# Linear attention beside a mixture of experts: numerators copied by ScalarE and multiplied by GpSimd, key-sum tails behind the queries' projection, eight steps a pair

## The chip, the cores and the metric

The kernel runs on one core of a Trainium2 chip. The metric is the time of one execution on the device in microseconds (us), as the median of several runs. One execution was also profiled; durations below come from that one.

## What is computed

```python
def _attn_ref(q, k, v, omega):                 # q, k, v: 4 x 8 heads x 576 x 64; omega: 128 x 64
    scale = 1.0 / np.sqrt(np.sqrt(D))
    def phi(x):
        h = np.einsum('bhsd,md->bhsm', x, omega) - np.sum(x * x, axis=-1, keepdims=True) / 2.0
        h = h - np.max(h, axis=-1, keepdims=True)
        return np.exp(h) / np.sqrt(m)
    q_p, k_p = phi(q * scale), phi(k * scale)
    kv = np.einsum('bhsm,bhsd->bhmd', k_p, v)  # key sums, and z: the same with ones for v
    num = np.einsum('bhsm,bhmd->bhsd', q_p, kv)
    den = np.einsum('bhsm,bhm->bhs', q_p, z)[..., None] + 1e-06
    return num / den

def _moe_ref(x, domain_probs, w1, w2):         # x: 2304 tokens x 512; 4 experts, 1024 hidden
    p = domain_probs / (domain_probs.sum(-1, keepdims=True) + 1e-09)
    for e in range(E):
        out += p[:, e:e + 1] * (np.maximum(x @ w1[e], 0.0) @ w2[e])
```

The 8 heads go in pairs, so there are 4 pairs a batch and 16 in all. A sequence of 576 is four tiles of 128 and a tail of 64.

## The kernel before

Attention and expert work are interleaved by hand: the order in the code is the order on every engine's queue. `emit` goes through the experts' visits (`plain`, later `fast`), and after each half tile of expert work it takes as many steps of an attention generator as a rate in `windows` says. The first batch is done by `Pair`; the twelve pairs of batches 1 to 3 by `Halves`. `later_ticks(pairs, over)` yields the steps of these: with `over` true for the eight pairs of batches 1 and 2, which run beside visit 3 up to N0 (76 steps for 45.4 shares of expert work), with `over` false for the four pairs of batch 3, beside the `fast` visits.

One pair of `Halves`, in before, takes nine steps. `project("k")` and `project_tails` (64-row matmuls, two heads in the two halves of the array, tiles k_ps and t_ps) come with `maxima`; then maxima of the tails, `bias` (nbk, from the squared lengths of `lengths` and the maxima) and `exp("k", 0)`; then `exp("k", 1)` and `exp_tails("k")`; then `project("q")` (q_ps); then the exponentials of the queries; then `sum_keys` (kv: one matmul for both heads' tails, 128 rows by 256 columns, and eight of 128 columns on the full tiles, then the parts kvh and kvl); then two steps of `turn` (transposes, qt_ps, into qth and qtl). With `over`, the `numerators` and `divide` of a pair are called in the first steps of the next pair (`before`): part 0 has 256 tokens a head, part 1 has 320. `numerators` makes numerator and denominator of a head in one PSUM tile nd, 64 partitions each, and ScalarE copies the denominators to dn; `divide` takes the reciprocal on VectorE and multiplies there, straight from nd, into raw_x, the experts' input.

All PSUM tiles come from one pool of eight banks (`bank`); a new tile waits until the bank that it gets has been read for the last time. nd needs one bank for part 0, two for part 1; k_ps, t_ps and q_ps two each; kv one; g of the experts one each.

ScalarE also makes the high parts of the split weights (w1sh, w1ah, w2h, sum), the relu hh and some of the accumulations; VectorE makes hl, the low part of the hidden values, and the accumulation acc; GpSimd makes the low parts of the weights and the squares of k and q. In the text, the pairs of the window with `over` count from the first to the eighth.

## Time and profile before

| | |
|---|---|
| median of 3 runs | 915.62 us (915.03 to 915.73) |
| the profiled execution | 915.08 us, span of its instructions 913.3 us |
| TensorE (PE) busy | 900.7 us, 99% |
| VectorE (DVE) busy | 556.7 us, 61% |
| ScalarE (ACT) busy | 433.3 us, 47% |
| GpSimd (POOL) busy | 378.6 us, 41% |
| PE waits, 58 to 276 us | 3.7 us in 6 waits |

A matmul's record ends later than the next begins, since they are pipelined; so how long PE spends on a kind of matmul is read from start to start. The idle time that the profile shows in brackets or in the list of waits begins at the modelled end of the matmul before. What releases a waiting instruction is named with its engine and line.

### The profile page before, as it was taken

To read this page: it belongs to the slowest core of one execution; us is meant where nothing else is said; L and a number is where in the kernel's file an instruction comes from. 1 tells how busy PE (TensorE), PEld (TensorE's weight loads), DVE (VectorE), ACT (ScalarE), POOL (GpSimd) and SP (SyncE) were. 2 spreads that over 40 slices of the span, in tenths; PEclk is the share of its full clock that TensorE was granted. 3 is DMA by queue.
4 is the path that set the end of the run, shared out by engine and by line. 5 is a ranking of instruction groups with operands and counts; after the bars stand their busy time and mean duration, and the time that the engine had idled before them with its cause. 6 is when DMAs were issued, how large, how long until landed. Compare 5 with 4: busy or idle time off the path is not lost.

```text
span 913.3 us, 13234 instructions
## 1 busy us (share of the span) xinstructions
PE 900.7 (99%) x4908; PEld 781.1 (86%) x4908; DVE 556.7 (61%) x946; ACT 433.3 (47%) x964; POOL 378.6 (41%) x296
## 2 busy tenths in 40 slices
PE   9999999999999999999999999999999999999998
PEld 9888888888777888888888889888888888898886
DVE  5755676777779655575757574886344545534543
ACT  6454665565664555445254445254544243342340
POOL 5756453444533453324344333344334343434330
PEclk9999999999999999999999999999999999999999
DMA  7663454444511612204122111214112112122102
GB/s 180 179 204 120 133 156 144 151 133 139 171 56 37 189 60 86 81 24 138 42 78 93 55 47 47 70 47 150 51 42 81 50 55 70 47 69 59 34 12 81
DMA packets 47360, 83.56 MB, mean 91 GB/s; under 512 B 8704, under 2 KB 17088, under 8 KB 47296
## 3 DMA queue, kind: packets, MB, share of 16 engines
q1 hardware_dynamic: 47056, 82.43, 29.9%
q8 instruction: 38, 0.62, 0.3%
q10 hardware_dynamic: 240, 0.30, 0.1%
q14 instruction: 26, 0.21, 0.1%
HBM read 77.99 MB, written 4.72 MB: 91 GB/s over the span
## 4 chain that ended last, share of the span: by engine, by line
PE 88%; DVE 7%; ACT 3%; issue 1%; DVEq 0%; ACTq 0%
PE g L713 28%; PE g L597 13%; PE g L599 13%; PE g L598 13%; PE g L582 3%; PE g L584 3%; PE g L583 3%; PE kv L316 2%; PE k_ps L265 1%; PE qt_ps L327 1%; PE k_ps L147 1%; ACT kp L298 1%; DVE dn L365 1%; PE kv L177 1%; PE q_ps L147 1%
## 5 line engine op out<-in xcount | busy, mean ns | idle before, releaser
L597 PE MATMUL g<-w2h,hh 128*128 128x512 f32 x536 | 212.4, 396 | 1.0 <-DVE raw_x L369 1.0
L599 PE MATMUL g<-w2h,hl 128*128 128x512 f32 x536 | 209.8, 391 | 1.2 <-DVE hl L589 1.2
L598 PE MATMUL g<-w2l,hh 128*128 128x512 f32 x536 | 209.0, 390 | 0.0
L494 POOL TENSOR_TENSOR w2l<-w2r,w2h 128x512 fp32r<-128x512 f32 x93 | 122.4, 1320 | 206.9 <-ACT w2h L491 145.9
L494 POOL TENSOR_TENSOR w1sl<-w1r,w1sh 128x1024 fp32r<-128x1024 f32 (+1 forms) x59 | 113.4, 1922 | 153.5 <-ACT w1sh L491 141.9
L610 DVE SCALAR_TENSOR_TENSOR acc<-g,pr,acc 128x512 f32<-128x512 f32 x126 | 93.7, 748 | 74.6 <-PE g L599 73.9
L724 DVE TENSOR_TENSOR sum<-g,sum 128x448 f32<-128x448 f32 x96 | 59.7, 622 | 117.7 <-PE g L713 110.1
L494 POOL TENSOR_TENSOR w1al<-w1r,w1ah 128x256 fp32r<-128x256 f32 (+1 forms) x77 | 82.5, 1090 | 110.3 <-ACT w1ah L491 110.3
L599 PEld LDWEIGHTS g<-w2h,hl 128*128 128x128 f32 x536 | 100.6, 188 | 24.5 <-DVE hl L589 2.4
L597 PEld LDWEIGHTS g<-w2h,hh 128*128 128x128 f32 x536 | 100.7, 188 | 21.1 <-PE nd L357 1.2
L598 PEld LDWEIGHTS g<-w2l,hh 128*128 128x128 f32 x536 | 100.8, 188 | 18.4
L725 ACT ACTIVATE hh<-sum 128x448 fp32r<-128x448 f32 x96 | 55.5, 578 | 121.9 <-DVE sum L724 121.9
L726 DVE SCALAR_TENSOR_TENSOR hl<-sum,hh 128x448 fp32r<-128x448 f32 x96 | 61.9, 644 | 61.9 <-ACT hh L725 61.9
L491 ACT ACTIVATE w1sh<-w1r 128x1024 fp32r<-128x1024 f32 (+1 forms) x59 | 51.0, 864 | 98.6 <-DVE w1r L548 98.4
L713 PE MATMUL g<-xbh,w1sh 128*128 128x448 f32 x256 | 93.6, 366 | 0.7 <-ACT sum L719 0.5
L713 PE MATMUL g<-xbl,w1sh 128*128 128x448 f32 x256 | 93.7, 366 | 0.0
L713 PE MATMUL g<-xbh,w1sl 128*128 128x448 f32 x256 | 93.4, 365 | 0.0
L719 ACT ACTIVATE sum<-g 128x448 f32<-128x448 f32 x96 | 51.7, 541 | 56.5 <-PE g L713 56.4
L713 PE MATMUL g<-xbh,w1ah 128*128 128x448 f32 x192 | 70.6, 367 | 0.9 <-ACT kp L298 0.9
L713 PE MATMUL g<-xbh,w1al 128*128 128x448 f32 x192 | 70.2, 366 | 0.0
L713 PE MATMUL g<-xbl,w1ah 128*128 128x448 f32 x192 | 70.1, 365 | 0.0
L491 ACT ACTIVATE w2h<-w2r 128x512 fp32r<-128x512 f32 x90 | 55.5, 624 | 8.8 <-issue 4.8
(161 smaller groups left out, 1603.8 us busy)
## 6 DMA issues: line engine op xcount, KB each, us to landing
w1r<-in_w SPq DMA_DIRECT2D x54, 512.0 KB, 3.7
w2r<-in_w SPq DMA_DIRECT2D x108, 256.0 KB, 2.6
out<-acc SPq DMA_DIRECT2D x18, 256.0 KB, 2.6
va<-in_vn SPq DMA_DIRECT2D x14, 256.0 KB, 4.1
k<-in_kd SPq DMA_DIRECT2D x12, 288.0 KB, 3.7
k<-in_kn SPq DMA_DIRECT2D x12, 288.0 KB, 4.3
q<-in_qd SPq DMA_DIRECT2D x12, 288.0 KB, 4.5
q<-in_qn SPq DMA_DIRECT2D x12, 288.0 KB, 4.8
```

The lines of the kernel that those rows point to most:

```text
L491: hi.activation(a, t, AF.Copy)
L494: lo.tensor_tensor(c, t, f32(a), ALU.subtract)
L582: nc.tensor.matmul(ps[:, :n], a[:, w], hi, start=(hp == 0), stop=False)
L597: nc.tensor.matmul(ps, ha[:, ts_], wa, start=(c == 0), stop=False)
L598: nc.tensor.matmul(ps, ha[:, ts_], wc, start=False, stop=False)
L599: nc.tensor.matmul(ps, hc[:, ts_], wa, start=False, stop=(c == FH - 1))
L610: nc.vector.scalar_tensor_tensor(acc[i], ps, sc, acc[i], ALU.mult, ALU.add)
L713: nc.tensor.matmul(ps, a[:, w], x[:, k], start=(start and k + at == 0), stop=(k == 1 and at == 2), skip_group_check=not start)
L719: nc.scalar.activation(t, P_[g][where], AF.Copy)
L724: nc.vector.tensor_tensor(t, P_[g][where], t, ALU.add)
L725: nc.scalar.activation(ha, t, AF.Relu)
L726: nc.vector.scalar_tensor_tensor(hc, t, 0.0, f32(ha), ALU.max, ALU.subtract)
```

## The change

`numerators` copies both halves of each nd to SBUF on ScalarE: the denominators to dn as before, and the numerators to a new tile nu, which shares its buffers with qth (part 1) and with qth and qtl (part 0). `divide` takes the reciprocal on VectorE and multiplies nu by dn on GpSimd, one instruction for 128 partitions where there were two for 64.

With `over`, the tails of the key sums are done apart, by `sum_tails`, directly behind `project("q")`: two 64-row matmuls of 128 columns, one a head, each into a bank of its own, where the eight matmuls of `sum_keys(False)` later add to them. kvh and kvl are then made in two instructions each. Without `over`, `sum_keys(True)` does what it did.

The steps are laid out anew. both `numerators` and both `divide` of the pair before move ahead by one step, `numerators(0)` into the step of `project("k")`; with `over` the exponentials of the keys' tails come ahead of the others, `sum_keys` and the values' load come with the first exponentials of the queries, and the keys' squares go to the step of `turn(0)`. A pair has eight steps with `over`, and the rate is 68 steps for the same 45.4 shares.

```diff
--- before.py
+++ after.py
@@ -305,18 +305,28 @@
                 nc.scalar.activation(f[rows, 0], self.t_ps[j][rows, cs], AF.Exp, bias=getattr(self, "nb" + which)[rows, 8:])
             (self.kp if which == "k" else self.qx)[2] = f
 
-        def sum_keys(self):
-
-
-            kv = bank("kv")[:, :VZ]
-            nc.tensor.matmul(kv, self.kp[2][:, 0], vb[:, self.hp], start=True, stop=False)
+        def sum_tails(self):
+
+            cs = [slice((1 - j) * P, (2 - j) * P) for j in range(2)]
+            self.kv = [(bank("kv")[:, :P], c) for c in cs]
             for j in range(2):
-                cs = slice((1 - j) * P, (2 - j) * P)
+                rows = slice(j * D, (j + 1) * D)
+                nc.tensor.matmul(self.kv[j][0], self.kp[2][rows, 0], vb[rows, self.hp, cs[j]], start=True, stop=False)
+
+        def sum_keys(self, tails):
+
+            if tails:
+                kv = bank("kv")[:, :VZ]
+                nc.tensor.matmul(kv, self.kp[2][:, 0], vb[:, self.hp], start=True, stop=False)
+                self.kv = [(kv[:, c], c) for c in (slice((1 - j) * P, (2 - j) * P) for j in range(2))]
+            for j, (ps, cs) in enumerate(self.kv):
                 for t in range(4):
-                    nc.tensor.matmul(kv[:, cs], self.kp[j][:, t], va[:, t, cs], start=False, stop=(j == 1 and t == 3))
+                    nc.tensor.matmul(ps, self.kp[j][:, t], va[:, t, cs], start=False, stop=(t == 3 and (j == 1 or not tails)))
             self.kv_h, self.kv_l = (att.tile([P, VZ], F32R, tag=x, name=x, bufs=1) for x in ("kvh", "kvl"))
-            nc.scalar.activation(self.kv_h, kv, AF.Copy, scale=1.0 / M)
-            nc.vector.scalar_tensor_tensor(self.kv_l, kv, 1.0 / M, f32(self.kv_h), ALU.mult, ALU.subtract)
+            for ps, cs in [(kv, slice(0, VZ))] if tails else self.kv:
+                hi, lo = self.kv_h[:, cs], self.kv_l[:, cs]
+                nc.scalar.activation(hi, ps, AF.Copy, scale=1.0 / M)
+                nc.vector.scalar_tensor_tensor(lo, ps, 1.0 / M, f32(hi), ALU.mult, ALU.subtract)
 
         def turn(self, part):
 
@@ -355,18 +365,18 @@
                 nc.tensor.matmul(ps[j], self.kv_h[:, w], qt_h[:, j], start=True, stop=False)
                 nc.tensor.matmul(ps[j], self.kv_l[:, w], qt_h[:, j], start=False, stop=False)
                 nc.tensor.matmul(ps[j], self.kv_h[:, w], qt_l[:, j], start=False, stop=True)
+            nu = att.tile([P, n], F32, tag="qth1" if part else "qt", name="nu", bufs=2 - part)
             for j in range(2):
                 own, other = slice(j * D, (j + 1) * D), slice((1 - j) * D, (2 - j) * D)
                 nc.scalar.activation(dn[own], ps[j][other], AF.Copy, bias=EPS)
-            self.num[part] = ps, dn, n
+                nc.scalar.activation(nu[own], ps[j][own], AF.Copy)
+            self.num[part] = nu, dn, n
 
         def divide(self, part):
-            ps, dn, n = self.num.pop(part)
+            nu, dn, n = self.num.pop(part)
             nc.vector.reciprocal(dn, dn)
             for o, c, m in in_ring(self.b * S + 2 * P * part, n):
-                for j in range(2):
-                    own = slice(j * D, (j + 1) * D)
-                    nc.vector.tensor_tensor(raw_x[own, place(self.hp), c:c + m], ps[j][own, o:o + m], dn[own, o:o + m], ALU.mult)
+                nc.gpsimd.tensor_tensor(raw_x[:, place(self.hp), c:c + m], nu[:, o:o + m], dn[:, o:o + m], ALU.mult)
 
     def opening(p):
 
@@ -385,35 +395,51 @@
         yield
 
     def later_ticks(pairs, over):
+
+        def after_sum(then):
+            if then:
+                then.load_v()
+                if then.hp == 0:
+                    then.load_tails()
+                if not over:
+                    then.square("k")
 
         before = None
         for p, then in zip(pairs, pairs[1:] + [None]):
             p.project("k")
             p.project_tails()
             p.maxima("k")
+            if before:
+                before.numerators(0)
             yield
             p.maxima_tails("k")
             p.maxima_tails("q")
             p.bias("k")
+            if over:
+                p.exp_tails("k")
             p.exp("k", 0)
-            if before:
-                before.numerators(0)
             p.lengths("q")
-            yield
-            p.exp("k", 1)
-            p.exp_tails("k")
             if before:
                 before.divide(0)
             yield
+            p.exp("k", 1)
+            if not over:
+                p.exp_tails("k")
+            if before:
+                before.numerators(1)
+            yield
             p.project("q")
             p.maxima("q")
+            if over:
+                p.sum_tails()
             if before:
-                before.numerators(1)
+                before.divide(1)
             yield
             p.bias("q")
             p.exp("q", 0)
-            if before:
-                before.divide(1)
+            if over:
+                p.sum_keys(False)
+                after_sum(then)
             if then:
                 then.load("k")
             yield
@@ -422,15 +448,13 @@
             if then:
                 then.load("q")
             yield
-            p.sum_keys()
-            if then:
-                then.load_v()
-                if then.hp == 0:
-                    then.load_tails()
-                then.square("k")
-            yield
+            if not over:
+                p.sum_keys(True)
+                after_sum(then)
+                yield
             p.turn(0)
             if over and then:
+                then.square("k")
                 then.square("q")
             yield
             p.turn(1)
@@ -1004,7 +1028,7 @@
         later = [Halves(b, hp) for b in range(1, B) for hp in range(NP)]
         windows = {
             0: (first_rest(pairs, opening(later[0])), 15 / 11),
-            3: (later_ticks(later[:-NP], True), 76 / 45.4),
+            3: (later_ticks(later[:-NP], True), 68 / 45.4),
             N0: (chain(opening(later[-NP]), later_ticks(later[-NP:], False)), 54 / (NV * (BIG // P + 1) * 0.8)),
         }
         ticks, n, done, per = iter(()), 0, 0.0, 0
```

PE, where the eighth pair's queries are projected (q_ps), before: the two parts of the numerators (nd, 320 columns) of the seventh pair follow it.

```order
L584 MATMUL g_3172<-xh,w1sl 128x512
L265 MATMUL q_ps<-om_r,q 128x128 x8
L355 MATMUL nd<-qth,kvh 128x320
L356 MATMUL nd<-qth,kvl 128x320
L357 MATMUL nd<-qtl,kvh 128x320
L355 MATMUL nd<-qth,kvh 128x320
L356 MATMUL nd<-qth,kvl 128x320
L357 MATMUL nd<-qtl,kvh 128x320
L582 MATMUL g_3172<-xh,w1sh 128x512
L583 MATMUL g_3172<-xl,w1sh 128x512
```

And now: the tails (kv, x2) follow it, and expert matmuls come next; the numerators stand six expert matmuls ahead of it.

```order
L606 MATMUL g_3240<-xh,w1sh 128x512
L607 MATMUL g_3240<-xl,w1sh 128x512
L608 MATMUL g_3240<-xh,w1sl 128x512
L265 MATMUL q_ps<-om_r,q 128x128 x8
L314 MATMUL kv<-vb,kp 128x128 x2
L606 MATMUL g_3240<-xh,w1sh 128x512
L607 MATMUL g_3240<-xl,w1sh 128x512
L608 MATMUL g_3240<-xh,w1sl 128x512
L606 MATMUL g_3240<-xh,w1sh 128x512
L607 MATMUL g_3240<-xl,w1sh 128x512
```

The numerators have left the place behind q_ps, and the tails have come there.

ScalarE, the same pair, from its keys' exponentials (kp) to the copies of the second numerators, before:

```order
L298 ACTIVATE kp<-k_ps,nbk 128x128 x4
L360 ACTIVATE dn<-nd 64x256 x2
L588 ACTIVATE hh<-g_3117 128x512
L491 ACTIVATE w1sh<-w1r 128x512
L298 ACTIVATE kp<-k_ps,nbk 128x128 x4
L305 ACTIVATE kp<-t_ps,nbk 64x128 x2
L360 ACTIVATE dn<-nd 64x320 x2
L588 ACTIVATE hh<-g_3172 128x512
L491 ACTIVATE w1sh<-w1r 128x512
```

And now (nu is the copied numerator; the copies of the first numerators stand ahead of this piece):

```order
L612 ACTIVATE hh<-g_3124 128x512
L515 ACTIVATE w1ah<-w1r 128x512
L305 ACTIVATE kp<-t_ps,nbk 64x128 x2
L298 ACTIVATE kp<-k_ps,nbk 128x128 x4
L612 ACTIVATE hh<-g_3182 128x512
L515 ACTIVATE w1sh<-w1r 128x512
L298 ACTIVATE kp<-k_ps,nbk 128x128 x4
L371 ACTIVATE dn<-nd 64x320
L372 ACTIVATE nu<-nd 64x320
L371 ACTIVATE dn<-nd 64x320
L372 ACTIVATE nu<-nd 64x320
L612 ACTIVATE hh<-g_3240 128x512
```

Four copies stand directly behind the second exponentials of the keys, and the tails' exponentials stand ahead of the first ones.

VectorE, the same pair, from the maxima of the keys to those of the queries, before:

```order
L589 SCALAR_TENSOR_TENSOR hl<-g_3057,hh 128x512
L281 TENSOR_REDUCE mxk<-k_ps 128x4 x2
L286 TENSOR_REDUCE mxk<-t_ps 64x1 x2
L286 TENSOR_REDUCE mxq<-t_ps 64x1 x2
L291 SCALAR_TENSOR_TENSOR mxk<-sqk,mxk 128x9
L292 SCALAR_TENSOR_TENSOR nbk<-sqk,mxk 128x9
L254 TENSOR_REDUCE sqq<-q 128x9
L589 SCALAR_TENSOR_TENSOR hl<-g_3117,hh 128x512
L365 RECIPROCAL dn<-dn 128x256
L369 TENSOR_TENSOR raw_x<-nd,dn 64x256 x2
L281 TENSOR_REDUCE mxq<-q_ps 128x4 x2
```

And now:

```order
L281 TENSOR_REDUCE mxk<-k_ps 128x4 x2
L613 SCALAR_TENSOR_TENSOR hl<-g_3124,hh 128x512
L286 TENSOR_REDUCE mxk<-t_ps 64x1 x2
L286 TENSOR_REDUCE mxq<-t_ps 64x1 x2
L291 SCALAR_TENSOR_TENSOR mxk<-sqk,mxk 128x9
L292 SCALAR_TENSOR_TENSOR nbk<-sqk,mxk 128x9
L254 TENSOR_REDUCE sqq<-q 128x9
L377 RECIPROCAL dn<-dn 128x256
L613 SCALAR_TENSOR_TENSOR hl<-g_3182,hh 128x512
L281 TENSOR_REDUCE mxq<-q_ps 128x4 x2
L377 RECIPROCAL dn<-dn 128x320
```

One hl of the experts has come to stand between the maxima of k_ps and those of t_ps, the products into raw_x are gone, and the reciprocal of the second numerators follows the queries' maxima.

## Rows read from the trace of the kernel before

**Rows 1.** The page: busy us, share of the span, instructions of each engine.

```profile
PE 900.7 (99%) x4908; PEld 781.1 (86%) x4908; DVE 556.7 (61%) x946; ACT 433.3 (47%) x964; POOL 378.6 (41%) x296
```

**Rows 2.** Waits of PE, 58 to 276 us: total us, times, longest.

```profile
PE kv L312 <- ACT qp L298: 1.0, 1, 1.0
PE g L597 <- DVE raw_x L369: 1.0, 1, 1.0
PE nd L355 <- DVE raw_x L369: 0.9, 1, 0.9
PE nd L355 <- ACT kp L298: 0.8, 3, 0.4
```

**Rows 3.** Timeline of PE, eighth pair: start us, us, line, tile, form, count, idle.

```profile
245.99 1.16 PE L265 MATMUL k_ps<-om_r,k 64*128 64x128 f32 x16
246.99 0.39 PE L274 MATMUL t_ps<-om_r,k 64*128 64x128 f32 x4
247.21 0.39 PE L274 MATMUL t_ps<-om_r,q 64*128 64x128 f32 x4
247.53 0.50 PE L582 MATMUL g<-xh,w1ah 128*128 128x512 f32 x1
...
249.02 0.28 PE L355 MATMUL nd<-qth,kvh 128*128 128x256 f32 x1
...
249.73 0.39 PE L582 MATMUL g<-xh,w1ah 128*128 128x512 f32 x1
...
252.54 1.16 PE L265 MATMUL q_ps<-om_r,q 64*128 64x128 f32 x16
253.67 0.42 PE L355 MATMUL nd<-qth,kvh 128*128 128x320 f32 x1
...
254.07 0.31 PE L357 MATMUL nd<-qtl,kvh 128*128 128x320 f32 x1
254.50 0.41 PE L355 MATMUL nd<-qth,kvh 128*128 128x320 f32 x1
```

**Rows 4.** Timeline of PE, key sums of the eighth pair.

```profile
261.78 0.70 PE L312 MATMUL kv<-vb,kp 128*128 128x256 f32 x2 [1.04 <-ACT qp L298]
262.32 1.95 PE L316 MATMUL kv<-va,kp 128*128 128x128 f32 x16
264.02 0.48 PE L597 MATMUL g<-w2h,hh 128*128 128x512 f32 x1
```

**Rows 5.** Timeline of VectorE, eighth pair.

```profile
247.40 1.28 DVE L281 TENSOR_REDUCE mxk<-k_ps 128x4 f32<-128x512 f32 x2
248.59 0.60 DVE L286 TENSOR_REDUCE mxk<-t_ps 64x1 f32<-64x128 f32 x2
...
250.13 0.75 DVE L254 TENSOR_REDUCE sqq<-q 128x9 f32<-128x576 f32 x1
252.93 0.69 DVE L589 SCALAR_TENSOR_TENSOR hl<-g,hh 128x512 fp32r<-128x512 f32 x1 [2.04 <-ACT hh L588]
253.54 1.74 DVE L365 RECIPROCAL dn<-dn 128x256 f32<-128x256 f32 x1
```

**Rows 6.** Timeline of ScalarE, eighth pair.

```profile
251.50 0.77 ACT L360 ACTIVATE dn<-nd 64x256 f32<-64x256 f32 x2
252.30 0.60 ACT L588 ACTIVATE hh<-g 128x512 fp32r<-128x512 f32 x1
252.79 0.62 ACT L491 ACTIVATE w1sh<-w1r 128x512 fp32r<-128x512 f32 x1
253.31 1.14 ACT L298 ACTIVATE kp<-k_ps,nbk 128x128 f32<-128x128 f32 x4
254.31 0.74 ACT L305 ACTIVATE kp<-t_ps,nbk 64x128 f32<-64x128 f32 x2
255.08 0.89 ACT L360 ACTIVATE dn<-nd 64x320 f32<-64x320 f32 x2
```

**Rows 7.** Groups of instructions, GpSimd, 58 to 276 us: count, busy us, mean ns.

```profile
L250 POOL TENSOR_TENSOR k<-k 128x576 f32<-128x576 f32 x8 | 9.2, 1148 | 3.5 <-DMA k<-in_kn 2.2 <-DMA q<-in_qd 1.2
```

More of the change, by code (lines that the diff above doesn't have):

```diff
@@ L407, in later_ticks @@
             yield
-            p.project("q")
-            p.maxima("q")
+            p.exp("k", 1)
+            if not over:
+                p.exp_tails("k")
             if before:
@@ L412, in later_ticks @@
             yield
+            p.project("q")
+            p.maxima("q")
+            if over:
[3 more added lines that the diff above has]
+            yield
             p.bias("q")
             p.exp("q", 0)
-            if before:
-                before.divide(1)
+            if over:
+                p.sum_keys(False)
+                after_sum(then)
             if then:
```

## Prediction

> **What bounds the kernel now.** I read the page's engine shares first, then who TensorE (PE) waits for in the stretch that the change touches, then the order of time of one pair there. PE is busy for 900.7 of 913.3 us [rows 1], so the time is PE's own work plus its waits; an engine beside it matters only where PE waits for it. In 58 to 276 us, where eight attention pairs are interleaved with the expert matmuls, PE waits six times for long: 1.0, 1.0, 0.9 and three that make 0.8, together 3.7 us [rows 2]. A wait costs a little more than its idle time, because the modelled end of the matmul before it hides some: two numerator matmuls stand 0.43 us apart (254.07 to 254.50) where 0.15 is usual, with 0.12 shown as idle [rows 3]. With some 0.16 for each of six, the waits are worth 3.7 + 1.0 = **4.7 us**. All are waits for one of eight PSUM banks: a numerators' bank was held until VectorE had divided (raw_x), or a bank with projections until ScalarE had taken the exponentials (kp, qp).
>
> **The change, part by part.**
>
> *Tails of the key sums.* Before, one 128-row matmul of 256 columns leads the block: 0.54 us to the next line, and the 8 matmuls of 128 columns behind it take 1.70, 0.21 each [rows 4]. So its work is 0.43 and the other 0.11 is the change of form at the block's entry, which the first of the 8 will pay instead. After, two 64-row matmuls of 128 columns follow the queries' projection, which has that form already. Two such (t_ps of the keys) take 0.22, 246.99 to 247.21 [rows 3]. Gain 0.43 - 0.22 = 0.21 a pair; bounds 0 (if the two don't overlap) and 0.32 (if the entry went too). Eight pairs: **-1.7 us**, bounds 0 and -2.6. The last four pairs keep the old form.
>
> *Numerators copied, GpSimd multiplies.* ScalarE gets two more copies a part. Two copies of 64x256 take 0.77, of 64x320 0.89 [rows 6], so a pair gets 1.66 us more on ScalarE. VectorE loses its multiplications. GpSimd gets 576 columns a pair; its 128x576 products take 1.15 [rows 7], in all 12 pairs 13.8 us beside 378.6 us of work [rows 1]. PE waits for none of these in itself. What changes is when banks come free: as soon as the copies are through, not after reciprocal and product. So the 4.7 us of old waits should go. **What is late next** is ScalarE: exponentials of the keys and four copies now stand in a row, and behind the projection of the queries the two tails need two banks of exactly these.
>
> The Trainium skill bears on this in TensorEngine Tiling, Restrictions and Gotchas: row tiles that work at once must write different PSUM banks, so packing costs banks. The trace of before agrees as far as it goes, since its 64-row matmuls also write two tiles; with one bank for both tails the second of the two waits below would not be there.
>
> *The new waits, for the eighth pair.* T counts from the start of its k_ps. PE: k_ps and t_ps 1.54; six numerator matmuls 0.71 and 0.1 for the form, 2.35; six expert matmuls at 0.23, 3.7; twelve, 6.5; six numerators of 320 at 0.15, 7.4; six more, 8.8; 0.1 for the form; q_ps from 8.9. The 0.23 is from 249.73 to 252.54, twelve and a change of form; the 0.1 from 247.53 to 249.02, 1.49 where six at 0.23 are 1.38; the 0.15 from 253.67 to 254.07, two and such a change [rows 3]. VectorE: both maxima start when k_ps is there and it has caught up, at 1.3, and take 1.2; then comes hl of g_3124, which ends on PE at 3.7 and whose relu on ScalarE lasts 0.5, so hl runs from 4.5 to 5.1; the tails' maxima and the bias take 1.54 (248.59 to 250.13) [rows 5], 6.7. ScalarE: tails 0.77, first exponentials 1.0, a relu 0.49, a split 0.52, second exponentials 1.0, one dn and one nu 0.89 [rows 6]: with 0.1 to start, 6.8, 7.6, 8.6, 9.1, 9.6, 10.6, 11.5. On PE the second tile of q_ps takes a bank that hl of g_3182 frees. VectorE has the queries' sum (0.7), a reciprocal (1.75) and hl (0.65) [rows 5] before that, and hl's relu ends at 9.2: 9.9 against 9.0, a wait of 0.9. q_ps then ends at 10.9; the second tail needs the bank of the first half's numerators, copied at 11.5: 0.6. Sum **1.5 us**.
>
> The other pairs by the same steps, from the order of the changed kernel (first pair: no numerators before it):
>
> | pair | VectorE held before the tails' maxima by | bias ready | PE waits at | us |
> |---|---|---|---|---|
> | 2 | acc of six g2 (PE ends 3.7) | 6.3 | first tail 0.55, second 0.65; acc and a split lie between the exponentials | 1.2 |
> | 3 | nothing | 4.0 | the turn, 0.1 | 0.1 |
> | 4 | acc of six g2 | 6.3 | q_ps, for the second exponentials | 0.4 |
> | 5 | hl of twelve short g1 (3.8) | 6.5 | q_ps 0.6 (an acc behind the reciprocal), second tail 0.6 | 1.2 |
> | 6 | nothing | 4.3 | nowhere: copies through at 10.05, needed at 10.2 | 0 |
> | 7 | hl of twelve short g1 | 6.5 | an expert bank 0.95 (first exponentials), q_ps 0.3, second tail 0.7 | 1.9 |
> | 8 | hl of six g1 | 6.7 | q_ps 0.9, second tail 0.6 | 1.5 |
>
> That is 6.3 us; 0.3 for the first pair and 0.2 at turns behind the reciprocal, which now stands ahead of the queries' bias (2.15 us for 320 columns there, estimated from 1.74 for 256 [rows 5]), make **6.8**. Bounds: 0.8 if VectorE is held in no pair, 13.8 if each of seven pairs waits the 1.9 of the seventh. I take 6.8 because the steps are those of rows 3, 5 and 6 and only their order is new.
>
> *Eight steps a pair.* 68 steps instead of 76 fill the same share of the expert work, so a step covers about 3.0 instead of 2.7 us and a pair lasts as long as before. The loads of keys move behind the values' load, which waits for the key sums; by that count they then have some 8 us until the next k_ps. The keys' squares move from the step of the key sums to the one behind it, so nearer to their lengths; by the same count as below, for the sixth pair, GpSimd is through near T = 21 of 24. Cost 0 under this cover; were a load late, its lateness would show as PE waiting for a DMA, which no row of [rows 2] does.
>
> *Last four pairs.* Copies and GpSimd products only; PE does not wait for numerators there before. I take 0, bounds -1 and +1.
>
> **Sum.** The profiled execution took 915.08 us (span 913.3): 915.08 - 1.7 - 4.7 + 6.8 = 915.5. It lies 0.5 below the median of the three runs, 915.62, so for a median **916.0**.
>
> **Rivals.**
> *Slower: ScalarE's queue before the tails.* Place: the second tail and the second tile of q_ps. In all seven pairs the expert work falls as in the seventh, and later expert relus queue behind the four copies. Price: from 6.8 towards 13.8 us of waits, 918 to 922, middle 919. It decides from 8.2 us of waits on. For it: VectorE is held by an expert instruction in five of seven pairs, and each 0.1 us there goes straight through ScalarE to PE; ScalarE carries 1.66 us more a pair. Against it: two pairs have room.
> *Faster: the chain has slack.* The relu and hl come earlier than I count, since I allow 0.2 to 0.3 us from a matmul's end to its relu, so that the tails' maxima are hardly held. Then the new waits fall to some 2 us: 915.6 - 1.7 - 4.7 + 2 = 911.2; with 0.8, 910. For it: pairs 3 and 6 have none. Against: in before, the same chain of the eighth pair ended 0.3 later than PE came, so slack was small there too.
> *GpSimd is late.* Its product waits for the reciprocal and holds the splits queued behind it, and the next turn's qth and qtl take over the slots of nu. In the eighth pair the product of 320 ends near T = 17, and the slot is wanted near 23. It decides from 6 us of lateness; price then that lateness a pair, a few us in all, about 919. The Trainium skill, GPSIMD Engine Reference, Engine selection, advises VectorE for elementwise products, with GpSimd about twice as slow on two inputs; in [rows 7] it takes 2.0 ns a column, and the 6 us absorb twice that.
> *The tails do not overlap* and cost what they did: 917.7.
>
> **How the numbers follow.** Forecast 0.43, slower by ScalarE's queue 0.30, chain with slack 0.25, GpSimd late 0.01, tails not overlapping 0.01. A measurement of this kernel can tell about 0.2%, 1.8 us: faster is below 913.8, slower above 917.4. So faster 0.25, same 0.43, slower 0.32. The forecast's own range is 913.8 to 917.4. The range reaches into both rivals, past the middle of the faster one and of the slower one, 911.0 to 920.0, and leaves out under 0.2.
>
> **What would show it.** Right: no PE wait for raw_x; PE waits at the lines of q_ps and of the tails for ScalarE (nu, kp) or for VectorE (hl, acc), in pairs 2, 4, 5, 7 and 8 and hardly in 3 and 6; the two tails take 0.22 us together where nothing holds them; the block of 8 begins 0.1 slower than it goes on. Wrong: waits of PE at the turn for qp, or for GpSimd or a DMA; waits in pairs 3 and 6; or none at the tails, which would mean that the bias is ready by 5.

## The result, and the profile after

The changed kernel takes 924.86 us (median of 6 runs, 923.17 to 927.46) beside 915.38 for the kernel before (914.65 to 915.9): 1.0106 times as long, 95% interval 1.0093 to 1.012. It is slower by about 1.1%, where 916.0 was forecast with a range from 911.0 to 920.0. The profiled execution took 924.77 us, with a span of 923.0 where the kernel before had 913.3, so the two traces show the whole difference: 9.7 us.

The page of the changed kernel, busy time of each engine, to be read against [rows 1]:

```profile
PE 905.0 (98%) x4924; PEld 783.3 (85%) x4924; DVE 540.3 (59%) x898; ACT 452.5 (49%) x1020; POOL 399.4 (43%) x324
```

VectorE lost 16 us, ScalarE and GpSimd gained 19 and 21, as the change says. PE's busy time rose by 4 us although its work hardly changed; the rest of the 9.7 us is idle. The granted clock of TensorE is 1.00 in every stretch of both traces, so the difference is not a slower clock. The difference arises where eight pairs are interleaved with the experts: from the first matmul of the first later pair to the first expert matmul of 448 columns it is 222.1 us against 212.4, worked out from the starts of the matmuls. So again, who PE waits for, from 58 to 310 us (total us, times, longest; line numbers of the changed kernel, where L314 is the tails, L337 the turn, L371 and L372 the copies dn and nu):

```profile
PE kv L314 <- ACT nu L372: 2.1, 5, 0.4
PE k_ps L265 <- DMA k<-in_kd: 1.7, 2, 1.2
PE kv L314 <- ACT kp L298: 1.1, 3, 0.5
PE g L621 <- ACT kp L298: 0.9, 1, 0.9
PE t_ps L274 <- DMA q<-in_qd: 0.9, 1, 0.9
PE q_ps L265 <- DVE hl L613: 0.7, 1, 0.7
PE q_ps L265 <- DVE acc L634: 0.7, 1, 0.7
PE qt_ps L337 <- ACT qp L298: 0.6, 2, 0.4
PE q_ps L265 <- ACT kp L298: 0.6, 1, 0.6
```

The waits of [rows 2] for raw_x and at the numerators are gone. In their place stand waits at the tails, at q_ps and at an expert bank, which the prediction has, and three kinds that it names as signs against itself or costs at almost nothing: two waits for a load of keys, one for a load of queries, and the turn.

**A held tail.** PE in the fifth pair (start us, us, line, tile, form, count, idle before and its releaser):

```profile
189.20 1.16 PE L265 MATMUL q_ps<-om_r,q 64*128 64x128 f32 x14 [0.69 <-DVE acc L634]
190.09 0.48 PE L314 MATMUL kv<-vb,kp 64*128 64x128 f32 x2
191.01 0.48 PE L314 MATMUL kv<-vb,kp 64*128 64x128 f32 x2 [0.43 <-ACT nu L372]
191.43 0.50 PE L621 MATMUL g<-w2h,hh 128*128 128x512 f32 x1
```

and ScalarE at the same time:

```profile
188.88 1.16 ACT L298 ACTIVATE kp<-k_ps,nbk 128x128 f32<-128x128 f32 x4
190.07 0.43 ACT L371 ACTIVATE dn<-nd 64x320 f32<-64x320 f32 x1
190.53 0.43 ACT L372 ACTIVATE nu<-nd 64x320 f32<-64x320 f32 x1
190.98 0.43 ACT L371 ACTIVATE dn<-nd 64x320 f32<-64x320 f32 x1
```

The first tail finds a bank; the second starts at 191.01, when nu has left its bank at 190.96. It is the wait that the hand chain of the prediction has. What the prediction lacks is the price: 0.43 us stand as idle, but from the first tail to the expert matmul behind the second it is 1.34 us, against 0.32 where nothing holds the tails (one pair of the run with loads early, by the starts of its matmuls). Held apart, the second starts 0.92 us behind the first, and the expert matmul 0.42 behind the second.

**A late load.** SyncE's queue before the fifth pair's turn (start us, us that the issue took, waiting included):

```profile
161.64 11.14 SPq L511 DMA_DIRECT2D w2r<-in_w  x3
172.88 0.39 SPq L128 DMA_DIRECT2D va<-in_vn  x1
...
174.62 0.54 SPq L246 DMA_DIRECT2D k<-in_kd  x1
```

```profile
178.13 1.16 PE L265 MATMUL k_ps<-om_r,k 64*128 64x128 f32 x16 [0.49 <-DMA k<-in_kd]
```

and the same place before:

```profile
152.64 14.37 SPq L487 DMA_DIRECT2D w2r<-in_w  x3
167.11 0.37 SPq L246 DMA_DIRECT2D k<-in_kd  x1
```

```profile
175.45 1.16 PE L265 MATMUL k_ps<-om_r,k 64*128 64x128 f32 x16
```

Before, the keys were issued at 167.11 for a k_ps that starts at 175.45, 8.3 us ahead. After, they stand behind the values, and the values behind three loads of weights that SyncE holds until GpSimd's splits free their buffers: they go at 174.62 for a k_ps at 178.13, 3.5 us ahead. In the eighth pair it is 249.01, 4.5 us ahead:

```profile
249.01 0.33 SPq L246 DMA_DIRECT2D k<-in_kd  x1
```

```profile
253.51 1.16 PE L265 MATMUL k_ps<-om_r,k 64*128 64x128 f32 x16 [1.18 <-DMA k<-in_kd]
```

What SyncE's queue waits for between 56 and 314 us (total us, times, longest): L511 are the loads of weights, L128 those of the values, whose buffer the key sums still read:

```profile
SPq L511 <- POOL w1sl L518: 76.2, 14, 15.6
SPq L511 <- POOL w2l L518: 51.8, 21, 6.6
...
SPq L128 <- PE kv L324: 6.4, 3, 4.1
```

And VectorE, at the lengths of the keys, waits for GpSimd's squares, in a row that the kernel before does not have:

```profile
DVE sqk L254 <- POOL k L250: 5.6, 5, 2.3
```

A late load therefore has two ways to PE: the projection itself, and GpSimd's square, then VectorE's lengths and bias, then ScalarE's exponentials and the banks that they hold. The second way is worked out from the order of the queues; no single wait of PE was followed back along all of it.

### The profile page after: what moved, and what is told of

The parts are those of the page before. It is cut to its first block, busy times and chain, and to the rows that moved or that the text cites. A ratio compares the mean times of both kernels' runs of the same rounds, so it can differ in the third digit from the quotient of the medians.

```text
span 923.0 us, 13257 instructions
## 1 busy us (share of the span) xinstructions
PE 905.0 (98%) x4924; PEld 783.3 (85%) x4924; DVE 540.3 (59%) x898; ACT 452.5 (49%) x1020; POOL 399.4 (43%) x324
## 4 chain that ended last, share of the span: by engine, by line
PE 82%; DVE 6%; ACT 5%; DMA 4%; issue 2%; POOL 1%; SPq 1%; POOLq 0%; DVEq 0%; ACTq 0%
PE g L737 29%; PE g L621 13%; PE g L623 13%; PE g L622 13%; PE g L606 2%; PE g L608 2%; PE g L607 2%; PE kv L324 2%; ACT kp L298 2%; DMA k<-in_kT 1%; DMA k<-in_kn 1%; PE k_ps L265 1%; PE qt_ps L337 1%; DVE xbl L518 1%; ACT dn L371 1%
```

## The experiments

The theory after the result: the copies do what they were forecast to do, and three other parts of the change cost more than they give: the loads' place, the early tails, and the turn in eight steps. The rival for each is that its wait is only the one that shows, and that another takes its place when it goes. Ratios are to the kernel before, timed in the same session; 0.1% is 0.92 us.

### Copies alone

The kernel before, in its own order and nine steps, with the copies to SBUF and GpSimd's product.

```diff
+            nu = att.tile([P, n], F32, tag="qth1" if part else "qt", name="nu", bufs=2 - part)
...
+                nc.scalar.activation(nu[own], ps[j][own], AF.Copy)
...
-                    nc.vector.tensor_tensor(raw_x[own, place(self.hp), c:c + m], ps[j][own, o:o + m], dn[own, o:o + m], ALU.mult)
+                nc.gpsimd.tensor_tensor(raw_x[:, place(self.hp), c:c + m], nu[:, o:o + m], dn[:, o:o + m], ALU.mult)
```

> The kernel before, with the copies to nu and the products on GpSimd alone; steps, tails and rate as before. If the loss is the tails' banks and the loads, both absent here, the two waits for raw_x (some 2 us) go and the time is about 913 (911 to 915). If the load on ScalarE and GpSimd is the cause in itself, exponentials and relus come late everywhere and it is 918 or more.

Measured: 911.22 us, ratio 0.9955 (0.994 to 0.997), 4.1 us faster. PE's longest waits from 58 to 310 us:

```profile
PE nd L355 <- DVE hl L589: 0.6, 1, 0.6
PE g L597 <- ACT kp L298: 0.5, 1, 0.5
```

No wait for raw_x is left, and the 1.0 and 0.9 of [rows 2] have no heir of their size. This version is faster than both kernels; the loss lies in the rest of the change.

### Copies, with the product on VectorE

The same, with one word changed, which tells the banks from the load on VectorE.

```diff
-                nc.gpsimd.tensor_tensor(raw_x[:, place(self.hp), c:c + m], nu[:, o:o + m], dn[:, o:o + m], ALU.mult)
+                nc.vector.tensor_tensor(raw_x[:, place(self.hp), c:c + m], nu[:, o:o + m], dn[:, o:o + m], ALU.mult)
```

> The kernel before with ScalarE's copies of the numerators, and the product of all 128 rows on VectorE from the copy in SBUF instead of on GpSimd; steps and key sums as before. If the gain of the copies alone (915.7 to 911.2 us) comes from banks that are free as soon as ScalarE has copied them, where the product runs matters little: 910.5 to 912.5. If it comes from work taken off VectorE, the gain falls away, since one product of 128 rows takes the place of two of 64 there: 914 to 916.

Measured: 913.4 us, ratio 0.9978 (0.9969 to 0.9988): between the two. Some 2 us of the gain come with the banks, and as much with the place of the product. It is not that VectorE is the slower at the product; the groups of products on VectorE here, and on GpSimd in the run with copies alone (count, busy us, mean ns):

```profile
L369 DVE TENSOR_TENSOR raw_x<-nu,dn 128x256 f32<-128x256 f32 (+1 forms) x16 | 12.8, 798 | 1.4
```

```profile
L369 POOL TENSOR_TENSOR raw_x<-nu,dn 128x256 f32<-128x256 f32 (+1 forms) x16 | 12.9, 806 | 17.6 <-DVE dn L367 14.8 <-ACT qp L298 2.4 <-PE nd L356 0.3
```

GPSIMD Engine Reference (Engine selection) of the Trainium skill, which the prediction weighs, has GpSimd about twice as slow on two inputs; for this product, 256 and 320 columns in SBUF, the two took the same, and the measurement decides.

What differs is what stands behind the product. Two of PE's waits in the run with the product on VectorE:

```profile
PE g L713 <- ACT kp L298: 1.2, 1, 1.2
PE g L597 <- ACT hh L588: 1.2, 1, 1.2
```

The first lies in the stretch of the last four pairs, at 461.54 us: reciprocals, products, accumulations and then the keys' maxima and bias stand on VectorE there with hardly a pause, and PE waits for the exponentials behind that bias. The kernel before has this wait too (0.9 us), the copies alone do not; and from the first expert matmul of 448 columns to the end of the span it is 617.2 us here, 617.1 before and 616.2 with the copies alone. So about 1.0 of the 2.2 us is relief of VectorE, behind the stretch that the prediction counts. The second wait (0.4 us with the copies alone) does not lead back to a product: VectorE's lengths of the keys had waited 0.78 us for GpSimd's square, and that for a load. How the other half reaches PE stays open.

### Loads early

The changed kernel; the next pair's loads are issued ahead of the key sums and the values, the keys' in the step of the queries' projection.

```diff
             if before:
                 before.divide(1)
+            if over and then:
+                then.load("k")
             yield
             p.bias("q")
             p.exp("q", 0)
+            if over and then:
+                then.load("q")
             if over:
                 p.sum_keys(False)
                 after_sum(then)
-            if then:
+            if not over and then:
                 then.load("k")
...
-            if then:
+            if not over and then:
                 then.load("q")
```

> The changed kernel with the load of the next keys one step earlier and that of the queries ahead of the key sums, so both ahead of the values' load and of some weight loads on SyncE's queue. If the late loads are a cost of their own, PE's waits for them (3.3 us with the cover) go: 921.5 (920.5 to 922.5). If PE only waits there because it would wait at the tails otherwise, 924 or more.

Measured: 917.59 us, ratio 1.0023 (1.0012 to 1.0034): 7.3 us less, more than twice the 2.6 us that PE's waits for a transfer show, and below the range expected. The bigger number fits the second way: the wait for GpSimd's square fell from 5.6 us to

```profile
DVE sqk L254 <- POOL k L250: 1.1, 4, 0.4
```

and the waits at the tails fell too, from 3.2 to 2.6 us:

```profile
L314 PE MATMUL kv<-vb,kp 64*128 64x128 f32 x32 | 6.2, 301 | 2.6 <-ACT nu L372 1.7 <-ACT kp L298 0.9
```

### The keys' load alone early

As above, with the queries' load left where the change puts it.

```diff
+            if over and then:
+                then.load("k")
             yield
             p.bias("q")
...
-            if then:
+            if not over and then:
                 then.load("k")
```

> The changed kernel with the load of the keys alone issued early, the queries' load left where the change puts it. The waits for a transfer were 1.7 us for the keys and 0.9 for the queries in the changed kernel, and both together early gave 7.3. If the late keys carry most of it, through GpSimd's square and VectorE's lengths, 918 to 920; if the queries' are as much, 921 to 922.5.

Measured: 918.34 us, ratio 1.0036 (1.0023 to 1.005). The keys early give back 6.5 of the 7.3 us, in line with the way over the square, for which VectorE waits 1.1 us here as well. Not all of it need be the keys': the queries' load has two issues fewer ahead of it in the queue, and PE's wait for it is gone too.

### The same place, another queue

Nothing is moved; the later pairs' loads are issued by ScalarE.

```diff
-                nc.sync.dma_start(t[:, i], src[which][self.b - 1, self.hp])
+                eng.dma_start(t[:, i], src[which][self.b - 1, self.hp])
...
-                then.load("k")
+                then.load("k", nc.scalar if over else nc.sync)
...
-                then.load("q")
+                then.load("q", nc.scalar if over else nc.sync)
```

> The changed kernel with nothing moved: the later pairs' loads of keys and queries stand where the change puts them, but are issued by ScalarE instead of SyncE. If they are late because SyncE's queue is held ahead of them (loads of weights that wait for GpSimd's splits, the values that wait for the key sums), most of the 7.3 us that the early loads gave back comes back, less what issuing four loads a pair costs ScalarE: 917.5 to 920. If their later place in the program is what makes them late, or the transfers take longer, 923 to 925.

Measured: 918.91 us, ratio 1.004 (1.0025 to 1.0055), 6 us less with the same place in the program. ScalarE's queue in the fifth pair, while SyncE still has the values to issue (its load of va goes at 170.98):

```profile
169.20 0.33 ACTq L246 DMA_DIRECT2D k<-in_kd  x1
169.58 0.44 ACTq L246 DMA_DIRECT2D k<-in_kn  x1
```

What was late was SyncE's queue: each load waits for what stands ahead of it there, whatever that waits for. The Trainium skill says where such a wait sits, in DMA: Bandwidth & Descriptors (Anatomy of one DMA): DMA engines do not wait for semaphores, the sequencer that issues does, ahead of the dispatch. The trace agrees: in the changed kernel SyncE took 11.14 us to issue three loads of weights.

The run with loads early is another 1.3 us faster. Part of that can be clock: in the profiled execution here the granted clock stood at 0.50 (1.2 GHz) from about 261.0 to 264.5 us, in that of the run with loads early at 1.00 throughout.

### Late loads in the kernel before

From the other side: the kernel before, with one edit.

```diff
-            if then:
+            if not over and then:
                 then.load("k")
...
-            if then:
+            if not over and then:
                 then.load("q")
...
             p.sum_keys()
             if then:
                 then.load_v()
                 if then.hp == 0:
                     then.load_tails()
+                if over:
+                    then.load("k")
+                    then.load("q")
                 then.square("k")
```

> The kernel before with one edit: the next pair's loads of keys and queries stand behind its load of values, a step or two later than they did. If late loads alone slow this kernel, without any other part of the change, the first transpose-side products wait for a transfer in some pairs and GpSimd's squares follow late: 919 to 923. If nine steps leave room enough for them, 915 to 916.5.

Measured: 943.32 us, ratio 1.0304 (1.0284 to 1.0323): 28 us from the place of the loads alone, far more than either theory has. PE's largest waits:

```profile
PE k_ps L265 <- DMA k<-in_kd: 7.7, 4, 4.6
PE q_ps L265 <- ACT kp L298: 2.6, 2, 1.9
PE nd L355 <- ACT kp L298: 2.5, 3, 1.2
PE nd L355 <- ACT kp L305: 1.8, 1, 1.8
```

The group of GpSimd's squares of keys, with its idle time before them, and VectorE's wait for them:

```profile
L250 POOL TENSOR_TENSOR k<-k 128x576 f32<-128x576 f32 x8 | 9.2, 1145 | 46.2 <-DMA k<-in_kn 32.8 <-issue 13.5
```

```profile
DVE sqk L254 <- POOL k L250: 19.6, 6, 6.4
```

In [rows 7] the squares waited 3.5 us. Here GpSimd stands 46 us before eight of them, and the splits queued behind them stand with it. In this run the squares of the keys stand in the step of their loads, in the changed kernel two steps behind, which would explain why it pays less; that was not tried by itself.

Not all of the 28 us is waiting. The two traces differ by 26.0 us, and 10.2 of these are PE's busy time, 910.9 us for 900.7, with the same matmuls. The granted clock, 1.00 throughout before, fell to 0.50 (1.2 GHz) in four stretches, from about 107.8, 172.7, 200.0 and 271.7 us on, of 3.4, 3.4, 6.8 and 3.4 us. PE had waited in or just ahead of each; ahead of the first it stood 4.6 us for a load of keys, and the k_ps behind it took 2.08 us instead of 1.16:

```profile
107.90 2.08 PE L265 MATMUL k_ps<-om_r,k 64*128 64x128 f32 x16 [4.57 <-DMA k<-in_kd]
```

Expert matmuls of 512 columns stand 0.43 us apart in these stretches and 0.23 outside. PE is busy for some 16 of the 17 us, so the clock makes about 7.5 of the 28 us (an estimate from these rows).

### Key sums whole, in eight steps

The changed kernel without the early tails: one matmul of 128 rows and 256 columns leads the block, as before.

```diff
-            if over:
-                p.sum_tails()
...
-                p.sum_keys(False)
+                p.sum_keys(True)
```

> The changed kernel with its key sums whole again: one 128-row matmul for the tails at the head of the block, in the same step; all else as changed. If the two tails' banks are the main cost, the 6.3 us by which their line grew go: 918.5 (917 to 920.5), with the late loads and the turns left. If ScalarE is simply late, the wait passes to the next tile that wants a bank: 923 or more.

Measured: 922.37 us, ratio 1.0077 (1.0062 to 1.0093): 2.5 us less (2.7 by the ratios, uncertain by 1.9), where some 6 were expected. The group of L314, 7.1 us busy and 3.2 idle in the changed kernel, became 4.7 busy without idle, but PE's waits moved on:

```profile
PE qt_ps L337 <- ACT qp L298: 2.4, 4, 1.2
PE k_ps L265 <- DVE qtl L348: 1.4, 1, 1.4
PE g L604 <- ACT kp L298: 0.8, 1, 0.8
```

Here the expectation was wrong: of the waiting that PE loses at the tails, part is found again at the turn (2.4 us, 0.6 in the changed kernel) and at the next k_ps. The late loads are not the reason for the small gain, since with the loads early it is as small (917.59 to 914.98, in the next run).

### Both, loads early and sums whole

```diff
-            if over:
-                p.sum_tails()
...
+            if over and then:
+                then.load("k")
...
+            if over and then:
+                then.load("q")
...
-                p.sum_keys(False)
+                p.sum_keys(True)
...
-            if then:
+            if not over and then:
                 then.load("k")
...
-            if then:
+            if not over and then:
                 then.load("q")
```

> The changed kernel with the next pair's loads issued early (as in the run with loads early, 917.6 us) and the key sums whole (as in the run with whole sums, 922.4 us). If the two costs are of their own and add, 924.9 - 7.3 - 2.5 = 915.1: 914.5 to 916. If both were one and the same wait, that gain is counted twice and the time stays at 917 to 918.

Measured: 914.98 us, ratio 0.9994 (0.9984 to 1.0003). The two add: 7.4 us from the loads with whole sums, 7.3 with early tails.

### Loads early, the two tails beside the block

The two tails keep their form and their banks; they stand in the step of the other eight products.

```diff
-            if over:
-                p.sum_tails()
...
             if over:
+                p.sum_tails()
                 p.sum_keys(False)
```

> The changed kernel with the loads issued early and the two tail products of 64 rows, still each in its own bank, standing directly ahead of the other eight products instead of behind the queries' projection. If the tails cost because their two banks are taken early, while ScalarE still has to copy numerators out of them, the banks are free by then and the time falls from 917.6 to 913 to 915.5. If the form itself costs (two accumulations, two more evictions), it stays at 917 to 918.

Measured: 915.55 us, ratio 0.9998 (0.9988 to 1.0007), 2 us less than with the tails early, and not told apart from the whole sums. The tails no longer wait:

```profile
L314 PE MATMUL kv<-vb,kp 64*128 64x128 f32 x32 | 3.9, 322 | 0.0
```

So what the early tails cost is their moment; two banks for them, once ScalarE has emptied these, hold nothing up. The two-tile form by itself gives nothing here. By the starts of the matmuls the tails take 0.42 us a pair, where the whole one takes 0.43; the block behind them takes 0.1 more than the 1.70 of [rows 4], and the first tail starts 0.1 us later behind its expert matmul than the whole one does (0.32 for 0.23), as PE goes into the form of 64 rows and out again.

### Nine steps with early tails

```diff
             p.bias("q")
             p.exp("q", 0)
-            if over:
-                p.sum_keys(False)
-                after_sum(then)
...
-            if not over:
-                p.sum_keys(True)
-                after_sum(then)
-                yield
+            p.sum_keys(not over)
+            after_sum(then)
+            yield
...
-            3: (later_ticks(later[:-NP], True), 68 / 45.4),
+            3: (later_ticks(later[:-NP], True), 76 / 45.4),
```

> The changed kernel with nine steps: the key sums of the full tiles in a step of their own behind the queries' exponentials, the values' load with them, 76 steps for the same share. The tails stay behind the queries' projection. If eight steps are the cause (loads, turns), those 3.3 and 2 us go: 919.5. If the tails' banks are, each pair reaches them some 0.8 us earlier against the same chain on ScalarE, 5 us more over the pairs, which eats that: 924 to 926.

Measured: 916.61 us, ratio 1.0016 (1.0006 to 1.0026). That is below both times expected; they count 3.3 us for late loads, where the run with loads early gave 7.3 back. The loads are ahead of the values again, and no wait at a turn is left, but the tails still wait:

```profile
PE kv L314 <- ACT nu L372: 1.5, 4, 0.4
PE kv L314 <- ACT kp L298: 1.3, 2, 0.9
```

### Nine steps with whole sums

The same, without the early tails: of the change only the copies, GpSimd's product, the numerators one step earlier, the order of the keys' exponentials and the keys' squares one step behind the key sums are left.

```diff
-            if over:
-                p.sum_tails()
...
-            p.sum_keys(not over)
+            p.sum_keys(True)
```

> The run with nine steps (916.6 us), with the key sums whole again, so that what is left of the change is the copies, the products on GpSimd and the numerators one step earlier. If early tails cost some 5 us in either order of steps, 911 to 912.5, the same as the copies alone. If the numerators' earlier place is what costs, 914.5 to 916.5.

Measured: 912.12 us, ratio 0.9961 (0.9947 to 0.9976). In nine steps the early tails cost 4.5 us (5.0 by the ratios), and the rest hardly differs from the copies alone. Part of the 4.5 is clock: in the profiled execution with early tails, PE waited 0.87 us at the second tail of the first pair and 0.55 behind it, and then the granted clock stood at 0.50 (1.2 GHz) from 93.0 to about 96.4 us, with seven expert matmuls 0.43 us apart instead of 0.23, some 1.5 us in all. With whole sums it stood at 1.00 there.

### Eight steps, the sums behind the last exponentials

The run with both, with the sums one step later, so that they lie between the queries' last exponentials and the turn.

```diff
             p.exp("q", 0)
             if over and then:
                 then.load("q")
-            if over:
-                p.sum_keys(True)
-                after_sum(then)
...
             p.exp("q", 1)
             p.exp_tails("q")
...
+            p.sum_keys(True)
+            after_sum(then)
             yield
             p.turn(0)
```

> The run with early loads and whole sums (915.0 us, eight steps), with the key sums one step later, behind the queries' last exponentials, ahead of the turn. If the 2.9 us between it and the nine steps are turns that come too soon behind the last exponentials, the sums now lie between them and the waits of the turn for qp fall: 912.3 to 913.5. If the shorter steps themselves cost, whatever lies where, 914.5 to 915.5.

Measured: 913.59 us, ratio 0.9983 (0.9973 to 0.9992). The group of the turn's transposes in the run with both, in this run, and in nine steps with whole sums (busy us, mean ns, idle):

```profile
L337 PE MATMUL qt_ps<-ident,qp 128*128 128x128 f32 x64 | 11.4, 281 | 1.4 <-ACT qp L298 1.2
```

```profile
L337 PE MATMUL qt_ps<-ident,qp 128*128 128x128 f32 x64 | 11.2, 281 | 0.5 <-ACT qp L298 0.4
```

```profile
L337 PE MATMUL qt_ps<-ident,qp 128*128 128x128 f32 x64 | 10.0, 275 | 0.0
```

Busy and idle together they are 12.8, 11.7 and 10.0 us. The 2.8 us between the first and the last are as much as the whole difference of the two runs (914.98 and 912.12). The place of the sums gives 1.1 us back at the turn, 1.0 by the ratios, which alone would not tell it from nothing (uncertain by 1.2); but from the first k_ps of the later pairs to the first matmul of 448 columns the three traces take 212.9, 211.7 and 210.1 us, the same steps as at the turn. The other 1.6 us, with the sums already between, stay open: the shorter steps, or ScalarE's copies of the sums.

## Why the prediction was wrong

The ratios make a ladder from the kernel before to the changed one, in which each rung adds one part: copies 0.9955, numerators a step earlier, with the exponentials' new order and the keys' squares a step later, 0.9961, eight steps 0.9994, loads behind the values 1.0077 and early tails 1.0106. In us of 915.4, with 1.4 to 1.9 us of uncertainty each (in another order the rungs change: early tails cost 4.5 us in nine steps):

| part | forecast | measured |
|---|---|---|
| copies, product on GpSimd: old waits gone | -4.7 | -4.1 |
| numerators a step earlier, exponentials, squares | in the new waits, squares 0 | +0.5 |
| eight steps: the turn | 0.2 | +3.0 |
| loads behind the values | 0 | **+7.6** |
| tails early, with the new waits | -1.7 + 6.6 | +2.7 |
| sum | +0.4 | +9.7 |

The new waits of the forecast do not all lie in the last rung, since those at q_ps and at the expert bank show already in nine steps with whole sums.

**The step that failed is the loads at no cost.** They cost 7.6 us. The prediction names the cover, "some 8 us until the next k_ps", and the sign against it, "waits of PE at the turn for qp, or for GpSimd or a DMA"; all of that came but the GpSimd one, which shows at VectorE instead. The 8 us were counted from the place of the issue in the program. They had to be counted on SyncE's queue, whose rows in the trace of before show three loads of weights taking 14.37 us to issue just ahead of the keys: a queue that is often held, and the change moves four issues a pair back in it. The margin in the fifth pair fell from 8.3 us to 3.5.

**Old waits gone: right in kind**, and in size (4.1 for 4.7) partly by luck. Of the 4.1 us, 3.3 arise beside the experts, where the 4.7 were forecast (212.4 to 209.1 us in the traces), and 1.0 behind, in the last four pairs, for which the prediction took 0 with bounds of 1 either way. With the product on VectorE some 2 us are left, so the banks alone gave about half of the forecast or less. The prediction put no value on the time that VectorE is spared, 24.5 us with the copies alone, because PE does not wait for a product in SBUF; PE waits, in one row shown above, for the exponentials behind a bias that stands behind it. GpSimd's part was undersized as well, 13.8 us where its busy time grew by 21 (0.81 us a product, two a pair).

**New waits: right in kind and nearly in size, in idle time.** By pair, from the second on, the waits at q_ps, at the tails and at an expert bank are 0.8, 1.0, 0.1, 1.7, 0.4, 1.3 and 1.3 us, 6.7 before rounding (forecast 1.2, 0.1, 0.4, 1.2, 0, 1.9, 1.5: 6.3). Pair 3, which was to have room, waited at both tails and behind them; in pair 6 the expert matmul behind the tails waited. That the sum fits so well is luck in part: single pairs miss by 0.9 us too little to 0.6 too much, and these waits include what late loads did to the chain. In the run with loads early the same waits make about 4.4 us.

**The tails: mis-sized.** They were to gain 0.21 us a pair by overlapping. Where nothing holds them they do (0.32 with the way out of the form); but in six of the eight pairs of the changed kernel the second is held, and it is then 1.3 us or more from the first to the expert matmul behind. The group of L314 is 10.3 us, busy and idle, where the whole form takes 4.7. The prediction names the bank rule of TensorEngine Tiling (Restrictions and Gotchas) in the Trainium skill, that different row tiles write to different PSUM banks; with two banks to find, the second is the one that ScalarE holds, in five of the six pairs for a copy. Early tails with a single bank were not tried. What comes back when the tails go is less, 2.5 us, since part of the waiting moves to the turn.

**The turn: missed.** 0.2 us were forecast from the reciprocal ahead of the bias. The eight steps took away the step that lay between the last exponentials and the turn, and the transposes there, busy and idle, take 2.8 us more over eight pairs. Putting the sums between gave 1.1 of these back; what makes the rest is not shown.

The rivals fare no better. *ScalarE's queue* named a place that does wait, but the waits there are the forecast's own, and loads and turn carry what is missing. *The chain has slack* falls. *The tails do not overlap* falls too: where nothing holds them the two take 0.32 us. *GpSimd late* comes near, with GpSimd late at the squares, for want of data, not at the products.

## What to carry to other kernels

When an edit moves a load, read the queue that issues it, from the row of the issue to the row of the first reader, and look at what the loads ahead of it wait for; the place in the program says little about the time. Price a late input by everyone who reads it: here PE's own waits for the loads were 2.6 us of the 7.3 that early loads gave back, and much of the rest fits the wait for GpSimd's square. And take a change of several parts apart before discarding it: one part of this one was worth 4.1 us, and the others cost 13.8.

## What was not expected of the hardware

Two matmuls on separate row tiles cost 0.32 us, with the way out of their form, when they start together; when the second had to wait 0.43 us for its bank, the two cost 1.0 us more. Only 0.43 of that stands as idle time, so waits between such matmuls have to be read by the starts, not by the idle column. And four issues of loads a pair, one or two steps later in SyncE's queue, cost 28 us in a kernel whose PE waits came to 3.7 us in that stretch. PE's idle time is not all of that price: in four stretches, 17 us together, with waits of up to 4.6 us in them or just ahead, TensorE worked at a granted clock of 0.50 (1.2 GHz), by estimate some 7.5 us more.
